# Values and half of the output weights on a second DMA queue, in a one-core attention decode kernel

## The chip, the cores and the metric

One core of a Trainium2 chip runs the program. The metric is the device time of one execution in microseconds (us); lower is better. Before the change it is 1333.47 us, the median of 3 runs (1333.34 to 1333.58).

## The reference, cut to what matters

One token for each of two sequences (B = 2) is decoded through 32 attention heads with 16384 cached keys and values of 128 numbers each, all bf16. A gated sum with a small MLP follows, whose matmuls the kernel runs first. The weights that the kernel loads are 33.6 MB.

```
q = x @ wq                                  # x: [2, 1, 1024], wq: [1024, 4096]
scores = einsum("bhqd,bhkd->bhqk", q, k_cache) * Dh**-0.5     # k_cache: [2, 32, 16384, 128]
p = softmax(scores);  o = einsum("bhqk,bhkd->bhqd", p, v_cache)
a = o @ wo                                  # wo: [4096, 1024]
b = mlp(x);  g = sigmoid(sum(x * gate_w));  out = g * a + (1 - g) * b
```

For each of the 64 pairs of sequence and head ("heads" from here on, g = 0 to 63) the kernel reads 4 MB of keys and 4 MB of values once: 537 MB of the 570 MB it reads in all. Nothing is used twice, so this is a kernel that streams memory.

## The kernel before

A helper records all operations in program order and emits them engine by engine, with semaphore waits. `ring` is a buffer in SBUF of four slots of 4 MB (128 partitions of 32 KB). All large loads stand in one list and are issued by SyncE, in order, each into the first slot that is free:

```
def pump():
    while dma_q and slot_free:
        key, fns = dma_q.pop(0)
        idx = next(iter(slot_free))
        waits = slot_free.pop(idx)              # events that must be over before the slot is overwritten
        slot_of[key] = idx
        for k, fn in enumerate(fns):
            dsem = s_ring[idx] if len(fns) == 1 else s_tail[k]
            dma_done[key] = dma_done[key, k] = pl.dma("sp", (lambda e, fn=fn, idx=idx: fn(e, idx)), dsem,
                                                      waits=waits if k == 0 else ())
# ... (cut)
def kv_src(T, g):
    h, b = g // 2, g % 2
    return T[b, h].rearrange("(p j) d -> p (j d)", p=P)      # 32 KB in one piece for each partition
def q_k(g): queue_load(("k", g), [lambda e, idx: e.dma_start(ring[:, idx, :], kv_src(A_k, g))])
def q_v(g): queue_load(("v", g), [lambda e, idx: e.dma_start(ring[:, idx, :], kv_src(A_v, g))])
# ... (cut)   order of the list: weights, k0, k1, v0, k2, v1, k3, v2, ..., k63, v62, v63, wo (two halves)
```

The last half of `wo` is loaded in six pieces (three of 1 MB, 512 KB, two of 256 KB), so that the matmuls left over after the last piece are few. What is done for head g, and when slots come free:

```
for g in range(G + 2):
    for u in range(NU):                       # scores of head g
        do_T(g, u)    # VectorE transposes 1/8 of the key slot in place
        do_S(g, u)    # TensorE: 4 matmuls; after the last one the key slot is released -> pump()
        if u == 1: do_ext(g - 2); do_OT(g - 2)
    do_rmax(g) ... do_exp(g); do_PT(g)        # softmax: VectorE, TensorE, ScalarE
    do_PV(g - 1)      # TensorE: 32 matmuls on the value slot, then it is released -> pump()
    do_accc(g - 1)    # ScalarE copies the accumulator
# then do_aproj(): 64 matmuls per half of wo, waiting for that half's (or piece's) landing
```

Of the kernel before, what the change touches and what calls it, by code (L numbers as in the profile page):

```python
# [110 lines left out]
def _split(n, k):  # L111
    out, s = [], 0
    while s < n:
        out.append((s, min(k, n - s)))
        s += k
    return out


def build_kernel(nc, A_x, A_k, A_v, A_wq, A_wo, B_w1, B_w2, B_w3, B_w4, gate_w, out, dbg=None):
    dbg = dbg or {}  # L120
    B, Sq, D = A_x.shape
    _, H, Sk, Dh = A_k.shape
    F = B_w3.shape[1]
    HD = H * Dh
# [7 lines left out]
    G = B * H  # L132
    NBD = D // P
    NBF = F // P
    NRS = 4
# [20 lines left out]
    with ExitStack() as st:  # L156
        block = st.enter_context(nc.Block())
        sb = lambda name, shape, dt: st.enter_context(nc.sbuf_tensor(name, shape, dt))
        ring = sb("ring", [P, NRS, SLOT], BF16)
# [54 lines left out]
        s_ring = [sem(f"dr{i}") for i in range(NRS)]  # L214
# [4 lines left out]
        s_tail = [sem(f"dtl{i}") for i in range(CPS + 2)]  # L219
        pl = _Plan(esems)  # L220
# [27 lines left out]
        for cg in range(4):  # L248
# [9 lines left out]
                    waits=(ev_rowm,), sig=True)  # L258
# [2 lines left out]
        ev_cab = pl.add("dve", lambda e: e.tensor_scalar(cAB[:, 1:2], rowv[:, :], -NEG_BIG, NEG_BIG, op0=ALU.mult, op1=ALU.add),  # L261
                        waits=(e0,), sig=True)

        dma_q = []
        dma_done = {}
        slot_of = {}
        slot_free = {i: () for i in range(NRS)}
# [4 lines left out]
        def ring_w(idx, nk, width):  # L272
            return ring[:, idx, 0:nk * width].rearrange("p (k n) -> p k n", k=nk)

        def queue_load(key, fns):
            dma_q.append((key, fns))

        def pump():
            while dma_q and slot_free:
                key, fns = dma_q.pop(0)  # L280
                idx = next(iter(slot_free))
                waits = slot_free.pop(idx)
                slot_of[key] = idx
                for k, fn in enumerate(fns):
                    dsem = s_ring[idx] if len(fns) == 1 else s_tail[k]
                    dma_done[key] = dma_done[key, k] = pl.dma("sp", (lambda e, fn=fn, idx=idx: fn(e, idx)), dsem,
                                                              waits=waits if k == 0 else ())

        def release(key, ev):
            idx = slot_of[key]  # L290
            assert idx not in slot_free
            slot_free[idx] = tuple(ev) if isinstance(ev, (tuple, list)) else (ev,)
            pump()
# [21 lines left out]
        wloads = {}  # L315
# [8 lines left out]
        wo_parts = _split(NCT, CPS)  # L324
        wo_chunks = []
        for pi, (k0, kn) in enumerate(wo_parts):
# [3 lines left out]
            else:  # L330
# [3 lines left out]
                for t, (c, r0, rn) in enumerate(parts):  # L334
                    wo_chunks.append(((("wo", pi), t), [(c, r0 + r) for r in range(rn)]))

        def q_load(key):
            queue_load(key, wloads[key])

        def kv_src(T, g):  # L340
            h, b = g // 2, g % 2
            return T[b, h].rearrange("(p j) d -> p (j d)", p=P)

        def q_k(g):
            queue_load(("k", g), [lambda e, idx: e.dma_start(ring[:, idx, :], kv_src(A_k, g))])

        def q_v(g):
            queue_load(("v", g), [lambda e, idx: e.dma_start(ring[:, idx, :], kv_src(A_v, g))])

        B5 = banks[5]  # L350
        c0 = 0
# [175 lines left out]
        key = ("w2", 0)  # L527
# [3 lines left out]
        for hi in range(NHI):  # L531
            key = ("w3", hi)
# [3 lines left out]
        for pi, (k0, kn) in enumerate(w4_parts):  # L536
            key = ("w4", pi)
# [7 lines left out]
        for qd in range(NQ):  # L545
            ev_xr = pl.dma("act", lambda e, qd=qd: e.dma_start(xrow[32 * qd:32 * qd + 2, :], A_x[:, 0, qd * DQ:(qd + 1) * DQ]), s_xr,
                           waits=(ev_xr0,))
        for hi in range(NHI):
            q_load(("wq", hi))
        for key in w_order:  # L550
            q_load(key)
        q_k(0)
        for g in range(1, G + 2):
            if g < G:
                q_k(g)
            if g - 1 < G:
                q_v(g - 1)
        for pi in range(len(wo_parts)):
            q_load(("wo", pi))
        pump()  # L560

        def xrow4(row, b_n, nb):
# [5 lines left out]
        for nb in range(NBD):  # L568
            last = pl.add("pe", lambda e, nb=nb: e.transpose(tr_ps[:, nb * 4:nb * 4 + 2], xrow4(xg_row, 2, nb), ident[0:2, 0:2]),
                          waits=(ev_x, ev_ident), sig=(nb == NBD - 1))  # L570
# [10 lines left out]
        for hi in range(NHI):  # L581
            key = ("wq", hi)
            ev_arr = arrived(key)
            wv = ring_w(slot_of[key], R4, HD)
            for r in range(R4):
                kc = hi * R4 + r
                for h in range(H):
                    lastmm = (h == H - 1)
                    def fn(e, h=h, r=r, kc=kc, wv=wv, first=first):
                        return e.matmul(q_ps[:, h, :], lhsT=wv[:, r, h * Dh:(h + 1) * Dh], rhs=xT_bf[:, kc, :],  # L590
                                        start=first, stop=(kc == NBD - 1), skip_group_check=True)
# [6 lines left out]
        for bp in range(NBP):  # L598
            evp = pl.add("pe", lambda e, bp=bp: e.matmul(q4_ps[:, bp, :], lhsT=PermQ[:, bp, :],
                                                        rhs=q_sb[:, :, :].rearrange("p h b -> p (h b)"), start=True, stop=True),  # L600
                         waits=(ev_q, ev_const, ev_r0), sig=(bp == NBP - 1))
# [3 lines left out]
        for nb in range(NBD):  # L605
            lastg = pl.add("pe", lambda e, nb=nb: e.transpose(gw_ps[:, nb, 0:1], xrow4(gw_row, 1, nb), ident[0:1, 0:1]),
                           waits=(ev_gw, ev_const), sig=(nb == NBD - 1))
# [108 lines left out]
        def do_l(g):  # L716
            pg = g % 2
            ev_l[g] = pl.add("pe", lambda e: e.matmul(l_ps, lhsT=ones_f[:, :], rhs=rowsum[:, pg:pg + 1], start=True, stop=True),  # L718
                             waits=(ev_P[g], ev_rc.get(g - 1)), sig=True)

        def do_rc(g):
            pg = g % 2
            ev_rc[g] = pl.add("dve", lambda e: e.reciprocal(recip[:, pg:pg + 1], l_ps), waits=(ev_l[g], ev_OT.get(g - 2)), sig=True)  # L723
# [33 lines left out]
        for g in range(G + 2):  # L757
# [14 lines left out]
                do_accc(g - 1)  # L772
            if g < G:
                do_l(g); do_rc(g)
        assert not dma_q, "unissued DMAs remain"

        ev_alast = do_aproj()
        ev_fin = pl.add("dve", lambda e: e.tensor_copy(orow[0:PR, :], rows_ps[0:PR, 0:DQ]), waits=(ev_alast,), sig=True)
        for b, eng in enumerate(("sp", "act")):
            ev_out = pl.dma(eng, lambda e, b=b: e.dma_start(out[b, 0, :].rearrange("(q n) -> q n", q=NQ), orow[b:PR:32, :]), s_out[b],  # L780
                            waits=(ev_fin,))
# [5 lines left out]
        def loop_of(name):  # L787
            first = pl.mark[GL][name]
            return first, pl.mark[GL + 2][name] - first, (GE - GL) // 2

        @block.gpsimd
        def _(e):
            pl.emit("pool", e)
# [12 lines left out]

        @block.scalar
        def _(e):
            pl.emit("act", e, loop_of("act"))



def bass_gated_mix__mha_block_cached__mixer_s_mlp__decode_kernel(
    nc: bass.Bass,
    A_x: bass.AP,
    A_k_cache: bass.AP,
    A_v_cache: bass.AP,
    A_wq: bass.AP,
    A_wo: bass.AP,
    B_x: bass.AP,  # L820
    B_w1: bass.AP,
    B_w2: bass.AP,
    B_w3: bass.AP,
    B_w4: bass.AP,
    gate_w: bass.AP,
    out: bass.AP,
):
    build_kernel(nc, A_x, A_k_cache, A_v_cache, A_wq, A_wo, B_w1, B_w2, B_w3, B_w4, gate_w, out)
# [28 lines left out]
```

## Time and profile before

| what | value | where it is read |
|---|---|---|
| time | 1333.47 us | the runs |
| bytes moved | 570.65 MB, mean 429 GB/s over the span | the page |
| DMA share and rate from 200 to 1200 us | 1.00 and 432 GB/s | table of stretches |
| TensorE, VectorE busy in the same stretch | 67%, 61% | table of stretches |
| a key load, issue to landing | 25.2 us median | list of DMA issues |

First the page of the kernel before: the busy share of the DMA engines in 40 slices in tenths, the DMA queues with packets, megabytes and share of the 16 engines, and the chain of work that ended last.

```profile
span 1331.4 us, 14124 instructions
...
DMA  9999999999999999999999999999999999999998
...
q1 hardware_dynamic: 21608, 570.44, 99.7%
...
DMA 64%; PE 25%; DVE 8%; issue 2%; SPq 0%; DVEq 0%; ACT 0%; POOL 0%
```

One queue (q1, SyncE's) carries all of it and keeps the engines busy 99.7% of the time. The table of stretches of the same kernel, with the start and end, the length, busy time of PE, PEld, DVE, ACT and POOL, the granted TensorE clock, the DMA share and GB/s:

```profile
200.00:1200.00 1000.00, 665.48 (x3688) 254.84 (x3689) 606.14 (x771) 70.16 (x153) 20.76 (x104) 0.81 1.00 432
```

The list of DMA issues of the kernel before, with the size of one and the median time from issue to landing:

```profile
ring<-in_A_k_cache_dram SPq DMA_DIRECT2D x64, 4096.0 KB, 25.2
ring<-in_A_v_cache_dram SPq DMA_DIRECT2D x64, 4096.0 KB, 31.2
```

A 4 MB load takes 9.7 us, so 25.2 us from issue to landing means that some 15 us of other loads were ahead of it. The queue does not run dry: the DMA share is 1.00 from 200 to 1200 us.

The end of the kernel before, from its timeline (start, length, engine, line, operation, count, and in brackets the idle time before it and what ended that):

```profile
1318.25 3.90 PE L748 MATMUL ps<-ring,OT_sb 128*2 128x256 bf16 x80 [4.72 <-DMA ring<-in_A_wo_dram]
1323.22 0.61 PE L748 MATMUL ps<-ring,OT_sb 128*2 128x256 bf16 x16 [1.07 <-DMA ring<-in_A_wo_dram]
1325.71 1.02 PE L748 MATMUL ps<-ring,OT_sb 128*2 128x256 bf16 x16 [1.88 <-DMA ring<-in_A_wo_dram]
1326.93 1.04 PE L748 MATMUL ps<-ring,OT_sb 128*2 128x256 bf16 x12 [0.20 <-DMA ring<-in_A_wo_dram]
1328.21 0.38 PE L748 MATMUL ps<-ring,OT_sb 128*2 128x256 bf16 x4 [0.25 <-DMA ring<-in_A_wo_dram]
1328.65 0.42 DVE L778 CAST orow<-ps 98x256 bf16<-98x256 f32 x1 [14.84 <-PE ps L748]
```

The projection follows the arriving weights piece by piece; after the last piece only 4 matmuls are left.

### The profile page before, as it was taken

The page shows a single profiled execution, that of the slowest core. Times are in us where ns is not written, and L with a number is a line of the kernel's source. Part 1 is how long each engine was busy: PE and PEld are TensorE (multiplying, and loading weights), DVE is VectorE, ACT ScalarE, POOL GpSimd, SP SyncE. Part 2 cuts the span into 40 slices and gives each one's busy share as a digit, 9 for nine tenths or more (in the row PEclk, how much of TensorE's full clock was granted, in tenths as well). Part 3 has the DMA queues.
Part 4 walks back from the last instruction along what each step waited for, and adds up shares of the span by engine and source line. Part 5 has one row for each costly group of instructions (what it writes and reads, how often), then busy time and mean ns, then how long its engine had stood idle before and what let it go on. Part 6 is the DMA issues. An engine that isn't in the chain of part 4 may idle for free.

```text
span 1331.4 us, 14124 instructions
## 1 busy us (share of the span) xinstructions
PE 860.8 (65%) x5466; PEld 343.8 (26%) x5466; DVE 762.6 (57%) x1000; ACT 89.7 (7%) x195; POOL 32.9 (2%) x161
## 2 busy tenths in 40 slices
PE   3466666667666666666766676676667666666765
PEld 3322222222222222222222222222222222222222
DVE  1076566566656656665665666566566656656661
ACT  0000000000000000000000000000000000000000
POOL 1000000000000000000000000000000000000000
PEclk9978887787888778778878878977787788778787
DMA  9999999999999999999999999999999999999998
GB/s 401 431 425 433 433 428 435 428 434 432 432 431 428 437 429 432 432 431 434 428 432 432 432 432 429 433 432 432 431 430 435 430 431 433 432 431 430 433 431 344
DMA packets 21652, 570.65 MB, mean 429 GB/s; under 512 B 2291, under 2 KB 2307, under 8 KB 2694
## 3 DMA queue, kind: packets, MB, share of 16 engines
q1 hardware_dynamic: 21608, 570.44, 99.7%
q8 instruction: 11, 0.18, 0.1%
q14 instruction: 3, 0.02, 0.0%
q10 hardware_dynamic: 30, 0.01, 0.0%
HBM read 570.44 MB, written 0.00 MB: 428 GB/s over the span
## 4 chain that ended last, share of the span: by engine, by line
DMA 64%; PE 25%; DVE 8%; issue 2%; SPq 0%; DVEq 0%; ACT 0%; POOL 0%
DMA ring<-in_A_k_cache_dram 61%; PE ps L644 23%; DVE ring L632 7%; DMA ring<-in_A_wo_dram 2%; DMA ring<-in_A_wq_dram 2%; DVE OTp L727 1%; PE ps L461 0%; PE ps L590 0%; SPq L312 0%; PE ps L711 0%; PE ps L490 0%; PE ps L383 0%; DVEq L71 0%; ACT P_sb L697 0%; POOL mv L424 0%
## 5 line engine op out<-in xcount | busy, mean ns | idle before, releaser
L644 PE MATMUL ps<-ring,Z 128*128 128x512 bf16 x2048 | 655.6, 480 | 326.0 <-DVE ring L632 320.2
L632 DVE STREAM_TRANSPOSE ring<-ring 128x1024 f32<-128x1024 f32 x512 | 591.0, 1212 | 117.3 <-DMA ring<-in_A_k_cache_dram 117.3
L644 PEld LDWEIGHTS ps<-ring,Z 128*128 128x128 bf16 x2048 | 216.6, 114 | 692.5 <-issue 376.3
L660 PE MATMUL ps<-ring,PT_sb 128*32 128x512 bf16 x2048 | 123.7, 384 | 2.3 <-DMA ring<-in_A_v_cache_dram 2.3
L697 ACT ACTIVATE P_sb<-ps,negm 128x512 bf16<-128x512 f32 x64 | 44.0, 688 | 1118.9 <-DVE negm L691 1118.9
L727 DVE TENSOR_SCALAR OTp<-ps,recip,gT 128x1 bf16<-128x1 f32 x64 | 17.9, 280 | 159.9 <-PE ps L711 159.9
L669 DVE TENSOR_REDUCE rA<-ps 128x1 f32<-128x512 f32 x64 | 44.2, 691 | 100.4 <-PE ps L644 100.4
L703 DVE STREAM_TRANSPOSE PT_sb<-P_sb 128x512 bf16<-128x512 bf16 x64 | 45.5, 711 | 54.1 <-ACT P_sb L697 54.1
L660 PEld LDWEIGHTS ps<-ring,PT_sb 128*32 128x32 bf16 x2048 | 49.3, 97 | 45.8 <-issue 3.8
L676 PE MATMUL ps<-ident,rmax_bf 128*1 128x128 bf16 x64 | 13.9, 217 | 66.2 <-DVE rmax_bf L671 66.2
L706 ACT ACTIVATE acc_sb<-ps 128x512 bf16<-128x512 f32 x64 | 38.2, 597 | 53.9 <-PE ps L660 53.9
L730 POOL COPY OT_sb<-OTp 128x1 bf16<-128x1 bf16 x64 | 11.9, 186 | 1204.1 <-DVE OTp L727 1204.1
L676 PEld LDWEIGHTS ps<-ident,rmax_bf 128*1 128x1 bf16 x64 | 5.1, 79 | 97.8 <-DVE rmax_bf L671 97.8
L681 DVE TENSOR_REDUCE m_sb<-ps 1x1 bf16<-1x128 bf16 x64 | 18.0, 281 | 19.7 <-PE ps L676 19.7
L711 PEld LDWEIGHTS ps<-dsel,acc_sb 128*128 128x128 bf16 x256 | 20.4, 118 | 33.7 <-issue 30.0
L691 DVE TENSOR_SCALAR negm<-ps,cAB 128x1 f32<-128x1 f32 x64 | 17.7, 277 | 17.2 <-PE ps L686 17.2
L686 PE MATMUL ps<-m_sb,ones_bf 1*128 1x1 bf16 x64 | 11.0, 172 | 24.0 <-DVE m_sb L681 24.0
L718 PEld LDWEIGHTS ps<-rowsum,ones_f 128*128 128x128 f32 x128 | 19.2, 189 | 28.0 <-issue 26.8
L718 PE MATMUL ps<-rowsum,ones_f 128*128 128x1 f32 x128 | 24.7, 262 | 1.2 <-ACT P_sb L697 1.2
L723 DVE RECIPROCAL recip<-ps 128x1 f32<-128x1 f32 x64 | 10.7, 168 | 19.9 <-PE ps L718 19.9
L590 PE MATMUL ps<-xT_bf,ring 128*128 128x2 bf16 x256 | 7.1, 165 | 17.8 <-DMA ring<-in_A_wq_dram 17.8
L711 PE MATMUL ps<-dsel,acc_sb 128*128 128x1 bf16 x256 | 17.5, 172 | 1.1 <-ACT acc_sb L706 1.1
(91 smaller groups left out, 122.9 us busy)
## 6 DMA issues: line engine op xcount, KB each, us to landing
ring<-in_A_k_cache_dram SPq DMA_DIRECT2D x64, 4096.0 KB, 25.2
ring<-in_A_v_cache_dram SPq DMA_DIRECT2D x64, 4096.0 KB, 31.2
ring<-in_A_wq_dram SPq DMA_DIRECT2D x2, 4096.0 KB, 17.5
ring<-in_B_w_dram SPq DMA_DIRECT2D x2, 3584.0 KB, 32.4
ring<-in_B_w_dram SPq DMA_DIRECT2D x1, 4096.0 KB, 28.3
ring<-in_A_wo_dram SPq DMA_DIRECT2D x1, 4096.0 KB, 32.2
ring<-in_B_w_dram SPq DMA_DIRECT2D x1, 3072.0 KB, 29.0
ring<-in_A_wo_dram SPq DMA_DIRECT2D x3, 1024.0 KB, 21.3
```

What stands on the lines that cost most here:

```text
L632: ev_T[(g, u)] = pl.add("dve", lambda e: e.transpose(ap, ap), waits=(arrived(("k", g)),), sig=True)
L644: ev = pl.add("pe", lambda e, bp=bp: e.matmul(S_ps(pg)[:, 0:NCOL], lhsT=Z[:, pg, bp, ZO - 2 * u:ZO - 2 * u + P], rhs=kv[:, :, bp // 2, :, ...
L660: ev = pl.add("pe", lambda e, jj=jj, hf=hf, cg=cg: e.matmul(acc_ps[32 * cg:32 * cg + 32, 0:512], lhsT=PT_sb[:, pg, 32 * jj:32 * jj + 32], ...
L669: e1 = pl.add("dve", lambda e: e.tensor_reduce(rA[:, pg:pg + 1], S_ps(pg)[:, 0:NCOL], axis=AX.X, op=ALU.max), waits=(ev_S[g],), sig=True)
L676: ev_mt[g] = pl.add("pe", lambda e: e.transpose(mt_ps, rmax_bf[:, pg:pg + 1], ident[:, :]), waits=(ev_rmax[g], ev_m.get(g - 1), ev_ident i ...
L681: ev_m[g] = pl.add("dve", lambda e: e.tensor_reduce(m_sb[0:1, pg:pg + 1], mt_ps, axis=AX.X, op=ALU.max), waits=(ev_mt[g], ev_mb.get(g - 2) ...
L697: ev_P[g] = pl.add("act", lambda e: e.activation(P_sb[:, pg, :], S_ps(pg)[:, 0:NCOL], ACT.Exp, bias=negm[:, pg:pg + 1], scale=scale, accum ...
L703: ev_PT[g] = pl.add("dve", lambda e: e.transpose(PT_sb[:, pg, :], P_sb[:, pg, :]), waits=(ev_P[g], ev_PV.get(g - 2)), sig=True)
L706: ev_accc[g] = pl.add("act", lambda e: e.activation(acc_sb[:, :], acc_ps[:, 0:512], ACT.Copy), waits=(ev_PV[g], ev_ext.get(g - 1)), sig=True)
L711: ev = pl.add("pe", lambda e, w=w: e.matmul(oT_ps, lhsT=acc_sb[:, w * P:(w + 1) * P], rhs=dsel[:, w:w + 1], start=(w == 0), stop=(w == 3)) ...
L718: ev_l[g] = pl.add("pe", lambda e: e.matmul(l_ps, lhsT=ones_f[:, :], rhs=rowsum[:, pg:pg + 1], start=True, stop=True), waits=(ev_P[g], ev_ ...
L727: ev_OT[g] = pl.add("dve", lambda e: e.tensor_scalar(OTp[:, pg:pg + 1], oT_ps, recip[:, pg:pg + 1], gT[:, pg:pg + 1], op0=ALU.mult, op1=AL ...
```

## The change

Keys and most weights stay on SyncE's queue; values and the last half of `wo` go to ScalarE's. The intent is that each of the 16 DMA engines has two rings with work, so that it is never idle. Slots become fixed: two for keys, two for values. V(0) also waits for K(0) to land.

```
-        dma_q = []
+        dma_q = {"sp": [], "act": []}
...
         def pump():
-            while dma_q and slot_free:
-                key, fns = dma_q.pop(0)
-                idx = next(iter(slot_free))
...
+            for eng, todo in dma_q.items():
+                while todo and todo[0][2] in slot_free and (todo[0][3] is None or todo[0][3] in dma_done):
+                    key, fns, idx, after = todo.pop(0)
...
+                        dma_done[key] = dma_done[key, k] = pl.dma(eng, (lambda e, fn=fn, idx=idx: fn(e, idx)), dsem,
+                                                                  waits=tuple(waits) + (dma_done.get(after),) if k == 0 else ())
...
-            queue_load(("v", g), [lambda e, idx: e.dma_start(ring[:, idx, :], kv_src(A_v, g))])
+            queue_load(("v", g), [lambda e, idx: e.dma_start(ring[:, idx, :], kv_src(A_v, g))], (n_w[0] + 2 + g % 2) % NRS, "act",
+                       ("k", 0) if g == 0 else None)
...
+        queue_load(("wo", 0), wloads[("wo", 0)], (n_w[0] + G % 2) % NRS)
+        queue_load(("wo", 1), wloads[("wo", 1)], (n_w[0] + (G + 1) % 2) % NRS, "act")
...
-            pl.emit("act", e, loop_of("act"))
+            pl.emit("act", e)
```

The last line means that ScalarE's program is written out in full and no longer as a loop.

More of the change, by code (lines that the diff above doesn't have):

```diff
@@ L273, in ring_w, with queue_load @@
             return ring[:, idx, 0:nk * width].rearrange("p (k n) -> p k n", k=nk)
-        def queue_load(key, fns):
-            dma_q.append((key, fns))
+        def queue_load(key, fns, idx, eng="sp", after=None):
+            dma_q[eng].append((key, fns, idx, after))
         def pump():
-            while dma_q and slot_free:
-                key, fns = dma_q.pop(0)
-                idx = next(iter(slot_free))
-                waits = slot_free.pop(idx)
-                slot_of[key] = idx
-                for k, fn in enumerate(fns):
-                    dsem = s_ring[idx] if len(fns) == 1 else s_tail[k]
-                    dma_done[key] = dma_done[key, k] = pl.dma("sp", (lambda e, fn=fn, idx=idx: fn(e, idx)), dsem,
-                                                              waits=waits if k == 0 else ())
+            for eng, todo in dma_q.items():
+                while todo and todo[0][2] in slot_free and (todo[0][3] is None or todo[0][3] in dma_done):
+                    key, fns, idx, after = todo.pop(0)
+                    waits = slot_free.pop(idx)
+                    slot_of[key] = idx
+                    for k, fn in enumerate(fns):
+                        dsem = s_ring[idx] if len(fns) == 1 else s_tail[k]
+                        dma_done[key] = dma_done[key, k] = pl.dma(eng, (lambda e, fn=fn, idx=idx: fn(e, idx)), dsem,
+                                                                  waits=tuple(waits) + (dma_done.get(after),) if k == 0 else ())
         def release(key, ev):
@@ L335, in build_kernel @@
                     wo_chunks.append(((("wo", pi), t), [(c, r0 + r) for r in range(rn)]))
+        n_w = [0]
         def q_load(key):
-            queue_load(key, wloads[key])
+            queue_load(key, wloads[key], n_w[0] % NRS)
+            n_w[0] += 1
         def kv_src(T, g):
@@ L344, in q_k @@
         def q_k(g):
-            queue_load(("k", g), [lambda e, idx: e.dma_start(ring[:, idx, :], kv_src(A_k, g))])
+            queue_load(("k", g), [lambda e, idx: e.dma_start(ring[:, idx, :], kv_src(A_k, g))], (n_w[0] + g % 2) % NRS)
         def q_v(g):
-            queue_load(("v", g), [lambda e, idx: e.dma_start(ring[:, idx, :], kv_src(A_v, g))])
+            queue_load(("v", g), [lambda e, idx: e.dma_start(ring[:, idx, :], kv_src(A_v, g))], (n_w[0] + 2 + g % 2) % NRS, "act",
+                       ("k", 0) if g == 0 else None)
         B5 = banks[5]
@@ L551, in build_kernel @@
             q_load(key)
-        q_k(0)
-        for g in range(1, G + 2):
-            if g < G:
-                q_k(g)
-            if g - 1 < G:
-                q_v(g - 1)
-        for pi in range(len(wo_parts)):
-            q_load(("wo", pi))
+        for g in range(G):
+            q_k(g)
+            q_v(g)
+        assert len(wo_parts) == 2
+        queue_load(("wo", 0), wloads[("wo", 0)], (n_w[0] + G % 2) % NRS)
+        queue_load(("wo", 1), wloads[("wo", 1)], (n_w[0] + (G + 1) % 2) % NRS, "act")
         pump()
@@ L774, in build_kernel @@
                 do_l(g); do_rc(g)
-        assert not dma_q, "unissued DMAs remain"
+        assert not any(dma_q.values()), "unissued DMAs remain"
         ev_alast = do_aproj()
```

## The prediction

> **What bounds the kernel now.** The 16 DMA engines. The page shows a DMA share of 9 tenths or more in all slices but the last and 570.65 MB at a mean of 429 GB/s; the table of stretches gives share 1.00 and 432 GB/s from 200 to 1200 us, with TensorE 67% and VectorE 61% busy. In the trace's packet records each engine runs 32 KB packets back to back: 1213 to 1225 ns, mean 1218, and after each 4 MB load a 4-byte semaphore packet of 9 ns and a 6 ns gap. A 4 MB load takes 8 x 1.218 + 0.015 = 9.76 us, a head (K and V) 19.5 us, 64 heads 1249 us. The ring never runs dry: a key load lands a median of 25.2 us after its issue (list of DMA issues), of which 9.8 are its own, so some 15 us of work are always queued.
>
> **What the change does.** No byte, matmul or VectorE operation is removed. 64 V issues and 6 wo issues move to ScalarE's queue; an issue takes SyncE 0.33 us; ScalarE is 7% busy, and a V issue waits for the same event as the accumulator copy behind it. V(0) waits for K(0) to land (73 us), while K(1) is queued already, so the engines stay fed.
>
> **Do two rings move bytes faster?** I expect not. [...] The trace holds a small test: near 24.5 us ScalarE's small packets (512 B, 27 ns) and semaphores alternate one by one with SyncE's 32 KB packets on two engines, and those stay at 1213 ns: no cost, no gain. From 8 KB (309 ns) and 32 KB (1213 ns) packets I work out 27.2 GB/s per engine plus 8 ns per packet. If the second ring hid that, the 5 ns of spread and the seams, the gain would be 1.2%, 16 us. The seams alone are 128 x 15 ns = 2 us.
>
> **Could it starve?** Estimate from the timeline: K(g+1) and V(g) land together every 19.5 us; scores take about 10 us, softmax and PV 4 more, so the K slot returns 10 us and the V slot 14 us after landing, while the other two loads last 19.5 us. Both rings always hold work.
>
> **The tail** gets slightly worse. Now wo's first half lands at 1318 us and its 64 matmuls run under the second half's load. With alternating packets (32 KB of V, 8 KB of wo) V(63) gets most of the bandwidth, then the halves of wo share it, and the first lands some 3 us before the end. The matmuls of L748 (80 took 3.9 us) bunch up there: estimate +2 to +3 us.
>
> **Time.** 1333.5 - 0..2 (seams) + 2.5 (tail), give or take a few ns per packet (5 ns are 5 us): 1335 us, 1327 to 1344. Faster by over 2%: 0.01; within: 0.95; slower: 0.04.
>
> **Checks after.** Two dynamic queues with about 298 and 273 MB; middle slices at 430 to 434 GB/s; K and V landing medians near 30 us; 32 KB packets near 1218 ns; last wo matmuls bunched.
>
> **What would make this wrong.** A cost per switch between rings when both carry 32 KB packets (50 ns would be +4%); hidden per-packet overhead (up to -1.2%); [...] V issues delayed on ScalarE.

Passages that no trace or run shows are cut out, here and in the experiments, and each cut is marked. 1333.5 less 0 to 2 (seams) plus 2.5 (tail) came to 1335 us. The 15 ns of a seam were read too high: in the records the next piece starts 6 ns after the start of the semaphore's 9 ns, so there is no gap of 6 ns behind it (experiment 7).

## The result, and the profile after

The changed kernel takes 1334.24 us (median of 4 runs, 1333.12 to 1335.25), the kernel before 1333.40 us in the same rounds. The ratio is 1.0006, 95% interval 0.9989 to 1.0023: the same. A ratio here is the mean time of one kernel's fast runs over that of the other's fast runs of the same rounds, so it is not quite the ratio of the medians. The range predicted was 1327 to 1344.

The page of the changed kernel:

```profile
span 1333.4 us, 13950 instructions
...
DMA  9999999999999999999999999999999999999997
...
q1 hardware_dynamic: 11528, 297.80, 52.0%
q10 hardware_dynamic: 10110, 272.65, 47.5%
...
DMA 65%; PE 23%; DVE 9%; issue 2%; DVEq 0%; POOL 0%; SPq 0%; ACT 0%
```

Two queues now share what one carried, and the sum of their shares, 99.5%, is what the one had. The table of stretches of the changed kernel shows the same rate in the middle:

```profile
200.00:1200.00 1000.00, 664.02 (x3713) 255.15 (x3712) 605.15 (x773) 71.56 (x156) 20.46 (x102) 0.81 1.00 432
```

The list of DMA issues of the changed kernel:

```profile
ring<-in_A_k_cache_dram SPq DMA_DIRECT2D x64, 4096.0 KB, 25.3
ring<-in_A_v_cache_dram ACTq DMA_DIRECT2D x64, 4096.0 KB, 28.8
```

The end of the changed kernel, from its timeline:

```profile
1323.99 6.53 PE L750 MATMUL ps<-ring,OT_sb 128*2 128x256 bf16 x128 [7.72 <-DMA ring<-in_A_wo_dram]
1330.58 0.42 DVE L780 CAST orow<-ps 98x256 bf16<-98x256 f32 x1 [14.04 <-PE ps L750]
```

All 128 matmuls of the projection now stand in one block, because the first half of `wo` lands late, at 1323.9 us and no longer at 1318.2. By the trace's packet records the last data of the rings ends at 1327.7 us before and 1327.9 after: nearly equal. The matmuls end at 1328.59 before and at 1330.52 after, 1.9 us later, and this is nearly all of the 2.0 us between the two profiled spans. (The profiled run of the changed kernel was the slowest of its four.)

The packet records also show how an engine serves two rings. They list one record per piece of contiguous data: its start in ns on the records' clock (the span of this run starts at 10.98 us on it, that of the kernel before at 10.96), how long it took, bytes, and queue. Four records in a row on one engine of the changed kernel (engines are told apart by the end of one meeting the start of the next):

```
600295  1218  32768  q10
601509  1218  32768  q1
602723  1221  32768  q10
603941     9      4  q1      (semaphore of a key load)
```

The engine takes one 32 KB piece from ScalarE's ring, one from SyncE's, and so on. (In a rough reconstruction of the 16 engines over 60 us, 87% of the unbroken runs from one ring were one piece long.) The turns went by pieces and not by bytes: from 1294 to 1308 us of the span, where SyncE's ring brings the first half of `wo` in 8 KB pieces and ScalarE's ring the last values in 32 KB pieces, 165 of the small and 143 of the large ones started, so that `wo` got about a fifth of the bytes. This is one reason why its first half lands late; from about 1310 us on it also shares the engines with the second half. Over 110 to 1270 us of the span the 32 KB pieces took 1217.17 ns on average before and 1217.16 ns after, and the rates were 432 GB/s in both. Two rings neither sped up these engines, which are busy throughout (share 1.00), nor slowed them down.

### The profile page after: what moved, and what is told of

It reads as the page before. It is cut to its first block, busy times and chain, and to the rows that moved or that the text cites. A ratio compares the mean times of both kernels' runs of the same rounds, so it can differ in the third digit from the quotient of the medians.

```text
span 1333.4 us, 13950 instructions
## 1 busy us (share of the span) xinstructions
PE 859.6 (64%) x5466; PEld 344.5 (26%) x5466; DVE 762.7 (57%) x1000; ACT 89.8 (7%) x195; POOL 33.0 (2%) x161
## 4 chain that ended last, share of the span: by engine, by line
DMA 65%; PE 23%; DVE 9%; issue 2%; DVEq 0%; POOL 0%; SPq 0%; ACT 0%
DMA ring<-in_A_k_cache_dram 61%; PE ps L646 22%; DVE ring L634 8%; DMA ring<-in_A_wo_dram 3%; DMA ring<-in_A_wq_dram 2%; DVE OTp L729 1%; PE ps L750 0%; PE ps L465 0%; PE ps L592 0%; PE ps L713 0%; PE ps L494 0%; PE ps L387 0%; DVEq L71 0%; POOL mv L428 0%; DVE orow L780 0%
## 5 line engine op out<-in xcount | busy, mean ns | idle before, releaser
L720 PE MATMUL ps<-rowsum,ones_f 128*128 128x1 f32 x128 | 24.5, 260 | 1.2 <-ACT P_sb L699 1.2
## 6 DMA issues: line engine op xcount, KB each, us to landing
ring<-in_A_k_cache_dram SPq DMA_DIRECT2D x64, 4096.0 KB, 25.3
ring<-in_A_v_cache_dram ACTq DMA_DIRECT2D x64, 4096.0 KB, 28.8
```

Source lines behind the costliest of these rows:

```text
L720: ev_l[g] = pl.add("pe", lambda e: e.matmul(l_ps, lhsT=ones_f[:, :], rhs=rowsum[:, pg:pg + 1], start=True, stop=True), waits=(ev_P[g], ev_ ...
```

## The experiments

All results were correct against the reference. The first four ran with 9 runs of the kernel before (median 1333.47 us); the next four (1333.24 us), the last four (1333.38 us).

### 1. The changed kernel again

No edit.

> The changed kernel unaltered, as the yardstick of this call. Theory A (the engines are the limit, a second ring neither helps nor harms the middle; only the tail is 0 to 2 us longer because the last matmuls of the output projection bunch up after the last landing): 1333.5 to 1335 us, ratio 1.000 to 1.0015, 32 KB packets with a mean of 1217 to 1218 ns. Rival B (a gain in the middle, given back by the tail): the same total, so this run alone doesn't tell them apart.

Measured: 1334.11 us (1333.82 to 1334.89, 5 runs), ratio 1.0007 (0.9993 to 1.0020). In its profile the block of 128 matmuls took 5.45 us, not 6.53, and the span was 1332.0 us. So the tail costs between half a microsecond and two, and its length changes from run to run. The granted clock was 0.50 from 1324 to 1328 us and 0.76 in the 4 us after that in the first profile, 0.58 and 1.00 in this one.

### 2. The tail undone: both halves of wo behind the last values

```
-  queue_load(("wo", 0), wloads[("wo", 0)], (n_w[0] + G % 2) % NRS)
+  queue_load(("wo", 0), wloads[("wo", 0)], (n_w[0] + G % 2) % NRS, "act")
```

> The changed kernel with both halves of wo on ScalarE's queue, behind the last V, so that the first half lands about 10 us before the second. Theory A: the last DMA data still ends near 1328.5 us of the span, the first half of wo lands near 1318 us, the matmuls of the projection end about 0.4 us after the last landing instead of 2; total as before, 1333.0 to 1333.7 us. Rival B (two rings gain 1 to 2 us in the middle and the tail takes them back): with the tail mended the gain shows, 1331 to 1332.5 us. Rival C (the tail's bunching is harmless because the clock or something else decides): same as the changed kernel, 1334 to 1335.

Measured: 1333.43 us (1333.23 to 1334.11), ratio to before 1.0001. The timeline of this run:

```profile
1318.16 4.02 PE L750 MATMUL ps<-ring,OT_sb 128*2 128x256 bf16 x80 [1.45 <-DMA ring<-in_A_wo_dram]
...
1328.15 0.38 PE L750 MATMUL ps<-ring,OT_sb 128*2 128x256 bf16 x4 [0.25 <-DMA ring<-in_A_wo_dram]
1328.58 0.42 DVE L780 CAST orow<-ps 98x256 bf16<-98x256 f32 x1 [11.58 <-PE ps L750]
```

The end is that of the kernel before, to 0.1 us, and so is the time. (The expectation's 1328.5 us for the last data came from placing the start of the span at 10.24 us on the records' clock; with the trace's own start it is 1327.7 here as before.) There was no gain hidden in the middle that the tail had taken back; rival B has nothing to stand on. Between this kernel and the changed one the medians differ by 0.7 us, which the intervals do not resolve alone; the timelines do.

### 3. The tail alone: the kernel before, with only the last half of wo on ScalarE

```
-  ... = pl.dma("sp", (lambda e, fn=fn, idx=idx: fn(e, idx)), dsem,
+  ... = pl.dma("act" if key == ("wo", 1) else "sp", (lambda e, fn=fn, idx=idx: fn(e, idx)), dsem,
```

> The kernel before with only the second half of wo issued by ScalarE; all keys and values stay on SyncE's queue. Theory A: the second half no longer queues behind the last V and the first half, shares the engines with them, and the first half lands last of all, within 1 us of the end of the data; all 128 projection matmuls [...] then follow the last landing: 1337 to 1340 us. If bunching costs nothing: 1333.5.

Measured: 1337.24 us (1336.85 to 1337.88), ratio 1.0029 (1.0016 to 1.0043). In its timeline:

```profile
1327.29 5.26 PE L748 MATMUL ps<-ring,OT_sb 128*2 128x256 bf16 x128 [12.86 <-DMA ring<-in_A_wo_dram]
1332.61 0.42 DVE L778 CAST orow<-ps 98x256 bf16<-98x256 f32 x1 [17.89 <-PE ps L748]
```

The rings' last data ends at 1327.9 us, nearly as before (1327.7), but the projection begins at 1327.3 and ends 4 us later than before. This is the larger dose of the same effect: the two loads, which had landed one after the other (the first half by 1318.2 us, the second at 1327.7), now land nearly together, at the time of the second (by 1327.3 and at 1327.9). That the engines take turns between the rings was read from the records of the changed kernel, above.

### 4. The changed kernel without the wait of V(0) for K(0)

```
-  ... (n_w[0] + 2 + g % 2) % NRS, "act",
-             ("k", 0) if g == 0 else None)
+  ... (n_w[0] + 2 + g % 2) % NRS, "act")
```

> The changed kernel without the wait of V(0) for K(0)'s landing. V(0) is issued near 59 us, shares the engines with K(0), which lands about 5 to 9 us later than 73 us. Theory A: the engines are never idle either way, so the total stays within 1 us of the changed kernel (1333 to 1335). Rival C (the staggered start costs what the rings gain): 2 us or more faster.

Measured: 1337.53 us (1336.47 to 1337.81), ratio to before 1.0028 (1.0014 to 1.0041): slower than the kernel before by 4 us (0.3%, clear of the noise), and my expectation failed. The table of stretches of this run (columns as above), and SyncE's issue of K(3):

```profile
108.00:110.00 2.00, 2.00 (x11) 0.90 (x10) 2.00 (x3) 0.00 (x0) 0.00 (x0) 1.00 0.72 311
110.00:112.00 2.00, 2.00 (x10) 0.71 (x9) 1.55 (x2) 0.00 (x0) 0.00 (x0) 1.00 0.19 82
112.00:114.00 2.00, 0.86 (x4) 0.17 (x2) 0.97 (x3) 0.00 (x0) 0.00 (x0) 1.00 0.67 180
114.00:116.00 2.00, 1.73 (x33) 0.86 (x33) 0.89 (x3) 0.78 (x2) 0.00 (x0) 1.00 0.76 311
116.00:118.00 2.00, 0.60 (x10) 0.30 (x3) 1.68 (x4) 0.60 (x1) 0.00 (x0) 1.00 0.76 328
118.00:120.00 2.00, 1.91 (x8) 0.70 (x9) 1.07 (x1) 0.00 (x0) 0.00 (x0) 1.00 1.14 492
...
112.68 0.33 SPq L348 DMA_DIRECT2D ring<-in_A_k_cache_dram  x1
```

The changed kernel, in its table of stretches:

```profile
110.00:120.00 10.00, 8.47 (x29) 3.14 (x28) 7.36 (x8) 0.00 (x0) 0.40 (x2) 0.59 1.01 436
```

There the DMA share stays at 1.01. Here it falls as low as 0.19. (The table books a piece where it starts, hence 1.14 in the last stretch.) With the packet records cut at the edges, 3.3 us of the engines' time are missing between 100 and 125 us. The reason stands in the timelines. K(0) shares the engines with V(0), so the first transposes start at 84.2 us and not at 73.2; the key slot, and with it the issue of K(2), comes 11 us later (94.8 us against 83.5), and V(2) is issued at 116.3 instead of 103.0. V(0), K(1) and V(1) have all landed, and K(2) alone is left to load; its last data ends at 111.7 us, while K(3), for which a key slot must come free, is issued at 112.7 and brings its first data at 113.6. In between the engines have nothing to do. So engines with two rings did run dry here (the share of 0.19, the 3.3 us missing), when what compute needs first was made to share with what it needs later. The wait that the change put in front of V(0) is worth 3.4 us (the difference of the medians, and about the engine time that is missing), and rival C is refuted: the staggered start does not cost, it pays.

### 5 and 6. Small pieces, one ring and two

Both kernels, with a head's keys dealt to the partitions so that each partition reads eight pieces of 4 KB. The same order is used for keys and values, so the softmax does not notice.

```
-  return T[b, h].rearrange("(p j) d -> p (j d)", p=P)
+  return T[b, h].rearrange("(c p j) d -> p c (j d)", c=8, p=P)
-  ... e.dma_start(ring[:, idx, :], kv_src(A_k, g))              # and the same for A_v
+  ... e.dma_start(ring[:, idx, :].rearrange("p (c m) -> p c m", c=8), kv_src(A_k, g))
```

> The kernel before with keys and values read in eight runs of 4 KB per partition (the keys are dealt to the partitions in another order, the same for K and V, so the result is unchanged). One ring, one issue per load. Estimate from the traces: a 4 KB packet took about 161 ns, 64 of them 10.3 us instead of 9.75, over 128 loads +70 us: 1395 to 1410 us.

> The changed kernel with the same 4 KB runs: two rings. Here the fixed 8 to 10 ns per packet is eight times as frequent. Theory A (the fixed part is in the engine, whichever ring the packet came from): within 0.3% of the one-ring run of the same packets. Rival B (two rings overlap the fixed part of one packet with the data of another): up to 64 us (4.5%) faster than the one-ring run. Rival D (changing ring costs something that 32 KB packets were too few to show, say 5 ns a packet): slower by 40 us.

Measured: one ring 1400.46 us (1400.38 to 1400.57), two rings 1401.27 us (1400.42 to 1402.35). The 4 KB pieces took 163.9 ns on average in both and the middle ran at 409.6 GB/s in both. The tables of stretches, one ring and then two:

```profile
130.00:1300.00 1170.00, 714.48 (x4104) 256.31 (x4104) 672.41 (x857) 78.42 (x171) 23.15 (x116) 0.90 1.03 410
130.00:1300.00 1170.00, 795.49 (x4104) 304.21 (x4104) 671.99 (x856) 78.42 (x171) 22.76 (x114) 0.75 1.03 410
```

(A share of 1.03 means that the records overlap a little: 163.9 ns each, one every 160 ns.) Small pieces cost 5%, as worked out from the packets, and a second ring gives none of it back and costs nothing itself, although the engines again changed ring after nearly every single piece (95% of the unbroken runs were one piece long, by the same rough reconstruction). Rivals B and D fall by a factor that the runs resolve well: 64 us or 40 us expected, 0.8 us measured.

### 7 and 8. Eight loads in place of one, one ring and two

```
-  queue_load(("k", g), [lambda e, idx: e.dma_start(ring[:, idx, :], kv_src(A_k, g))])
+  queue_load(("k", g), [lambda e, idx, m=m: e.dma_start(ring[:, idx, m*(SLOT//8):(m+1)*(SLOT//8)],
+                                 kv_src(A_k, g)[:, m*(SLOT//8):(m+1)*(SLOT//8)]) for m in range(8)])
   # the same for values; all eight count on the slot's semaphore
```

> The kernel before with each K and V load cut into eight loads of 512 KB (4 KB per partition), so eight times the semaphore packets (9 ns and a 6 ns gap) beside the 4 KB packets. Expected against the one-ring run with 4 KB runs: + 7 x 15 ns x 128 loads = 13 us. Issue: 8 x 0.33 us per load, 5.3 of 20.7 us per head, no limit.

> The same eight loads with two rings. Theory A: within 0.3% of the one-ring run of the same loads. Rival B2 (the second ring fills the seams between loads): 13 us (0.9%) faster than it, and B (also the packets' fixed part) up to 75 us faster.

Measured: one ring 1402.88 us (1402.85 to 1402.91), two rings 1402.18 us (1401.17 to 1402.97). The two are the same. The 13 us for eight times as many semaphore packets did not come: 2.4 us did, and none of it in the middle, where the rate is again 409.6 GB/s and the 4 KB pieces took 163.2 ns instead of 163.9. The trace of the kernel before does not show 15 ns either: from the start of one 32 KB piece to that of the next on an engine it is 1213.6 ns on average, and 1219.9 with a semaphore between them, so a seam adds about 6 ns. My reading of the seams as a cost of 2 us in the kernel before (128 x 15 ns) was not supported. Where the 2.4 us went I did not find, except that they arise at the end: by 1380 us the two one-ring runs had moved the same bytes to within 0.05 MB, or 0.1 us.

### 9 to 12. Where issuing is the limit: 32 and 64 loads in place of one

As in 7 and 8, with 32 and 64 in place of 8 (with 64, the first 32 count on a second semaphore per slot, and readers wait for both). The reading that the last text names, that a second issuer saves issue time and nothing else, was what I supposed; no run had shown it before these.

> The kernel before with each K and V load cut into 32 loads of 128 KB (1 KB per partition). [...] Free issues took 0.33 to 0.45 us in the traces, so 32 of them 10.6 to 14 us per load and 21 to 28 us per head on one sequencer. Data, estimated from 27.2 GB/s and 8 to 10 ns a packet: 256 packets of 47 ns and 32 seams of 15 ns are 12.5 us per load, 25 us per head. About the knee: 1600 to 1900 us.

> The same 32 loads with two issuers: data-bound at 25 us a head, 1600 to 1680 us, so between equal and 12% faster than the one-ring run. If ScalarE's blocked issues hold up the exponentials it could also be slower than the one-ring run.

> 64 loads of 64 KB per K and V (512 B per partition), one issuer: 128 issues a head at 0.33 to 0.45 us are 42 to 58 us a head; data 512 packets of 27 to 29 ns and 64 seams are 15 to 16 us per load, 31 us per head. Issue-bound: 2700 to 3700 us, DMA share about 0.6 to 0.75 in the middle.

> The same with two issuers: each has 64 issues a head, 21 to 29 us, below the 31 us of data: 2000 to 2400 us, at least 20% faster than the one-ring run. If the second ring still gained nothing here, the reading that it only saves issue time would be wrong too.

| loads per 4 MB | one ring, us | two rings, us |
|---|---|---|
| 1 | 1333.40 | 1334.24 |
| 8 | 1402.88 | 1402.18 |
| 32 | 2045.40 | 2055.11 |
| 64 | 3990.49 | 2937.47 |

The rows come from different calls, in which the kernel before took 1333.24 to 1333.40 us. All four runs with 32 and 64 loads lie above the ranges that I had expected. What came true is "at least 20% faster" with 64 loads, and the caution that two issuers could be slower with 32.

The timeline of SyncE with 64 loads and one ring shows the issues end to end:

```profile
1005.03 30.56 SPq L346 DMA_DIRECT2D ring<-in_A_k_cache_dram  x64
1035.63 30.33 SPq L349 DMA_DIRECT2D ring<-in_A_v_cache_dram  x64
```

From one issue to the next it takes 0.48 us here, not the 0.33 to 0.45 that I had carried over, so a head takes 61 us. Its chain of waits is SyncE's queue:

```profile
SPq 89%; issue 9%; DMA 1%; PE 0%; DVE 0%
```

With two issuers the time falls by 26%, less than I expected. The timeline of ScalarE with 64 loads and two rings tells why:

```profile
1013.39 30.94 ACTq L352 DMA_DIRECT2D ring<-in_A_v_cache_dram  x64
1044.38 0.60 ACT L709 ACTIVATE acc_sb<-ps 128x512 bf16<-128x512 f32 x1 [31.83 <-issue]
1056.20 0.69 ACT L700 ACTIVATE P_sb<-ps,negm 128x512 bf16<-128x512 f32 x1 [11.22 <-DVE negm L694]
...
1057.81 2.27 ACTq L352 DMA_DIRECT2D ring<-in_A_v_cache_dram  x5
```

ScalarE issues for 31 us, and only then copies the accumulator and computes the next head's exponentials, 13.5 us in which it issues nothing and mostly waits for that head's scores. The period is 1057.81 - 1013.39 = 44.4 us, and the chain of waits is ScalarE's queue at 61%. With 32 loads two issuers are no faster, because the two costs happen to balance: one issuer needs 2 x 15.1 us per head; ScalarE's issues (17.0 us) and its share of the softmax come to 30.5 us.

This is the only place where a second issuer gained anything, and it gained by issue time: one sequencer issued for 61 us per head, and with two the period was 44.4 us. With 4 MB a load, SyncE's issues took 0.33 us each and it waited the rest of the time.

## Why the prediction was right

- **The bound.** Right. Before and after, the middle has a DMA share of 1.00 and 432 GB/s, and small pieces (experiments 5 to 8) move the time with the rate on one ring and on two.
- **Two rings move bytes no faster.** Right. Pieces of 1217.17 and 1217.16 ns, pieces of 163.9 and 163.9 ns, and totals within 0.1% of each other for 32 KB and for 4 KB pieces. The small test that it rested on lies 13.6 us after the start of the span; I gave its time on the records' clock, 24.5 us.
- **No starvation.** Right for the change as it is, by a smaller margin than I gave. I took the key slot to return 10 us after landing. In the changed kernel a key tile landed by 615.08 us and its scores ended at 628.43: 13.4 us, since the transposes of VectorE wait in the middle for an earlier head. With two key slots, two periods of 19.5 us less 13.4 leave 25.6 us from issue to landing; the median was 25.3, not near 30 (values: 28.8). Experiment 4 shows what happens without the staggered start, which I had taken for a detail.
- **The seams, 0 to 2 us gained.** Not seen. The middle's rate is unchanged, and in experiment 7 eight times the seams cost the middle nothing (409.6 GB/s in experiments 5 and 7).
- **The tail, +2 to +3 us.** The mechanism is right: undone it goes (experiment 2), alone and enlarged it costs 4 us (experiment 3). Its size was too large: 1.9 us in one profile and about 0.6 us in another, 0.6 to 0.8 us between the medians. I had the right matmuls bunched but took one speed for them; the block took 6.53 us in one run and 5.45 in the other. The granted clock was lower in the first (0.50 against 0.58 from 1324 to 1328 us, then 0.76 against 1.00), and I did not isolate that.
- **The sum.** 1335 predicted, 1334.24 measured. Two terms were too large and of opposite sign, which flattered the sum.

## What to carry to other kernels

Before giving a load to a second queue, look whether the DMA engines are ever idle and whether the issuing sequencer is: with engines at a share of 1.00 and a sequencer that mostly waits, a second ring changed here only the order in which loads land. That order mattered at the two ends (3.4 us in experiment 4, 4 us in experiment 3): the rings took turns piece by piece (165 pieces of 8 KB started beside 143 of 32 KB), so in a kernel like this one what is needed first (the first keys, the first half of the last weights) should not run beside what is needed later. A second issuer paid where issue time was the limit (64 loads, 26%), and less than expected, because ScalarE's issues held up the softmax work behind them. An engine without such work might be the better issuer; no run here tried one.

## Other measurements of issues, landings and pieces

- An issue took 0.33 us for a single 4 MB load, and 0.47 to 0.48 us in SyncE's long series of 128 KB and 64 KB loads (15.14 us for 32, 30.56 us for 64).
- An issue could take far longer. With 4 KB pieces and one ring, a value load's issue held SyncE for 9.6 to 10.6 us (three between 590 and 640 us), and in experiment 8 eight issues held ScalarE for 6.2 us. What held them was not shown. With 32 KB pieces no key or value load's issue took more than 0.44 us, before and after.
- Sharing the engines between rings delayed the earlier of two loads: the first half of `wo` from 1318.2 to 1327.3 us, which cost 4 us at the end (experiment 3), and K(0), whose transposes started at 84.2 us in place of 73.2, which cost 3.4 us at the start (experiment 4).
- Pieces of 4 and 8 KB took at least 159 and 309 ns in the kernel before, and those of 32 KB between 110 and 1270 us at least 1213. I work out 27.2 GB/s per engine and about 8 ns for each piece from these; a second ring did not hide the 8 ns (163.9 ns on average for 4 KB on one ring and on two).
